# Dealing a second MLP's hidden units unevenly: ten full blocks of w2 and three more on 32 partitions

## The chip, the cores and the metric

The kernel runs on one core of a Trainium2 chip. The metric is the time of one execution on the device in microseconds, the median over runs. Before the change it was 671.67 us, from three runs between 671.4 and 671.77.

## The reference

One token passes through two identical pairs of layers, attention over a cache and then an MLP, all in float32. Both pairs use the same weights and the same cache.

```
D, F = 512, 1376;  H, S, Dh = 32, 4096, 128
attention(x): q = (x @ wq) as 32 heads of 128
              p = softmax(q . k_cache / sqrt(128)), over 4096 keys
              return (p . v_cache, heads joined) @ wo
mlp(x):       h = gelu(x @ w1 + b1)      # 512 -> 1376
              return h @ w2 + b2         # 1376 -> 512
x = x + attention(layernorm(x));  x = x + mlp(layernorm(x))     # twice
```

Each cache is 32 x 4096 x 128 floats, 67 MB. They are read for each layer, save for what stays on the chip between the two layers, so 285 MB cross from HBM in one execution.

## The kernel before

The 32 heads are eight groups of four. For a group the kernel loads a block of K (128 partitions x 16384 floats), one of V of the same size and a pair of weight tiles. They go to one large tile `arena`, in which three homes of 32 blocks of U = 512 columns (`A_AT`, `C_AT`, `B_AT`) are used in turn. All loads are issued on SP's queue by `load` (L108), in program order. The first layer takes the groups upwards, the second downwards.

Each transfer from SP signals its landing on one of eight semaphores, taken in turn (`DMAHW0` to `DMAHW7` in the orders below), so a transfer also waits until the one eight places before it has landed. TensorE's matmuls are held in program order by `matmul` (L113), and nearly all of them have this line in the profile.

A vector for TensorE stands as a column on the partitions. The 1376 hidden units of the MLP are four bands of `FJ` = 344, and band j is made on partitions 32j of a PSUM tile: in `mlp` (L334), for each of the four row blocks c of w1 and each band j, one matmul of 344 columns (L340). Its two output rows are the products with x and the sums of w1's columns, from which the layer norm is made good afterwards. A transpose in blocks of 32 (L353) turns each band so that its units stand on 32 partitions, 11 columns of them: unit 32c + r of band j is on partition 32j + r, column c. A band of 344 fills ten columns and 24 units of the eleventh, so 8 of 352 places are padding with zeros in w2 and b1. Two vector instructions and a gelu on ScalarE (L358 to L362) give `g`, 128 x 11, and then 11 blocks of w2 follow, each 128 partitions x 512 columns: block c is multiplied by column c of g in four matmuls of 128 columns, one for each quarter of the outputs (L365 to L368), accumulated in PSUM.

Padding in w2 is loaded with it: 128 rows of 11 x 2 KB, 2816 KB.

`idle` (L199) issues a matmul by zeros, with no use for its result; a 512-column one stands behind the gelu's inputs and one behind the fourth block of w2 (L374).

At the program's end, after the last group's V, SP issues wo, w1 in three transfers (`W1_AT_END`) and w2 in four (`W2_AT_END`: blocks 0 to 3, 4 to 7, 8 and 9, 10), L583 to L587. The destination is home A, w2 from its block 11 on. TensorE then makes the attention's output, w1's products as they land, and w2's products as they land; a last transpose (L184), an addition (L593) and a store of 2 KB (L594) end the program. The first MLP, in the middle of the program, runs through the same function with its own transfers and with fillers of its own.

Of the kernel before, what the change touches and what calls it, by code (L numbers as in the profile page):

```python
# [14 lines left out]
ALU = mybir.AluOpType  # L15
AX = mybir.AxisListType

P = 128
D = 512
H, S, DH = 32, 4096, 128  # L20
F = 1376
G = 8
J = 4
C = 8
FJ = F // J
FB = 11
W1C = FJ * J
EPS = 1e-5
U = 512
NC = 4 * U  # L30
# [7 lines left out]
A_AT, B_AT, C_AT = RING  # L38
# [4 lines left out]
SCRATCH = SHARED + 10 * U  # L43
# [11 lines left out]
W1_AT_END = ((0, 2), (2, 3), (3, 4))  # L55
LAST = ((0, 4), (4, 6), (6, 7), (7, 8))
W2_AT_CHANGE = (0, W1C, 2 * W1C, 3 * W1C, 10 * U, 11 * U)
W2_AT_END = (0, 4 * U, 8 * U, 10 * U, 11 * U)


@with_exitstack
def decode_layers(ctx: ExitStack, tc: tile.TileContext, vectors, k, v, w, w1, w2, out):
    nc = tc.nc
# [3 lines left out]
    def ctile(name, *shape):  # L67
        return const.tile([P, *shape], F32, name=name)
# [6 lines left out]
    cells = ctile("cells", CELLS)  # L75
# [3 lines left out]
    gelu = WIDE + 33  # L79
# [5 lines left out]
    def small(name, n=1):  # L85
        nonlocal first_front, rest
        if name.startswith("gelu_"):
            i = "hug".index(name[-1])
            return cells[:, gelu + FB * i : gelu + FB * (i + 1)]
        if name not in places:  # L90
            fit = [j for j in range(J) if gaps[j] + n <= ends[j]]
            if name in ("by_dma", "ready", "m"):
                places[name] = front, first_front, n
                first_front += n
            elif fit:
                places[name] = cells, gaps[fit[0]], n
                gaps[fit[0]] += n
            else:
                places[name] = cells, rest, n
                rest += n  # L100
        t, a, m = places[name]
        assert m == n and first_front <= FRONT and rest <= CELLS
        return t[:, a : a + n]

    def at(first, n):
        return arena[:, first : first + n]

    def load(first, src):  # L108
        t = at(first, src.shape[-1])
        tc.keep_in_program_order(nc.sync.dma_start(t, src))  # L110
        return t

    def matmul(*a, **kw):  # L113
        tc.keep_in_program_order(nc.tensor.matmul(*a, **kw))  # L114

    def activation(*a, **kw):
        tc.keep_in_program_order(nc.scalar.activation(*a, **kw))  # L117
# [14 lines left out]
    wq_t = by_four(load(SHARED, of_w(1, 0, 1)))  # L132
    nc.vector.memset(wide, 1.0)
    nc.vector.memset(cells[:, WIDE:], 0.0)
    by_dma = small("by_dma", FB + 8)
    b1c, b2c, xcol = by_dma[:, :FB], by_dma[:, FB : FB + 4], by_dma[:, FB + 4 :]
    nc.scalar.dma_start(by_dma, vectors)

    make_identity(nc, ident)
# [9 lines left out]
    pS, pO = (psum.tile([P, 512], F32, name=n) for n in ("pS", "pO"))  # L149
# [10 lines left out]
    zero = zq[:, :4]  # L160
# [4 lines left out]
    def of_32(t, n, i=0):  # L165
        return t[:, : 32 * n].rearrange("p (c q) -> p c q", q=32)[:, :, i]
# [4 lines left out]
    def pairs(t):  # L171
        return t[:, :8].rearrange("p (c i) -> p c i", i=2)
# [23 lines left out]
                nc.gpsimd.tensor_copy(pairs(t[:, 32 * j :])[:, :, 0], x)  # L196
        return t, s

    def idle(to, n=U, of=C_AT, amid=False):  # L199
        matmul(to[:, :n], zero[:, 0:1].to_broadcast([P, P]), at(of, n), start=not amid, stop=not amid)  # L200

    def idle_aside(n):
        for _ in range(n):
            idle(pM[:, ASIDE:], U - ASIDE)
# [6 lines left out]
    def mean_of(xs, s):  # L211
        nm = minus_mean(s, 0)
        xc, sq, ss, negm = small("xc", 4), small("sq", 4), small("ss"), small("negm")
        nc.vector.tensor_scalar(xc, pairs(xs)[:, :, 0], nm, None, op0=ALU.add)
        nc.vector.scalar_tensor_tensor(sq, xc, 1.0, xc, op0=ALU.mult, op1=ALU.mult, accum_out=ss)
        nc.vector.tensor_copy(negm, nm)
        return negm, ss

    def rstd_of(ss):
        nv = minus_mean(ss, 1)  # L220
        ve, r = small("ve"), small("rstd")
        nc.vector.tensor_scalar(ve, nv, -1.0, EPS, op0=ALU.mult, op1=ALU.add)
        if pM is pS:
            nc.vector.memset(pS[:, U - 2 :], 0.0)
        nc.gpsimd.tensor_tensor(r, ve, power, op=ALU.pow)
        return r
# [104 lines left out]
    def get_ready_for(function):  # L331
        activation(small("ready"), one, function)

    def mlp(xs, s, w1_t, w2_t, load_w2=None, behind_w2=None):  # L334
        get_ready_for(AF.Gelu_apprx_tanh)
        xb = small("xb", 4)
        nc.gpsimd.tensor_tensor(xb, pairs(xs)[:, :, 0], b2c, op=ALU.add)
        for c in range(4):
            for j in range(J):
                matmul(pO[32 * j : 32 * j + 2, :FJ], pairs(xs)[:, c, :], w1_t[c][:, FJ * j : FJ * (j + 1)],  # L340
                       start=(c == 0), stop=(c == 3))
            if c == 0:
                nm, ss = mean_of(xs, s)
            if c == 1:
                r = rstd_of(ss)
            if load_w2:
                load_w2(c)
                for _ in range(min(c + 1, 2) if c < 3 else 0):
                    idle(pO[:, 3 * P :], P, amid=True)
        if pS is not pO:  # L350
            idle(pS)
        ht = at(SCRATCH, 32 * FB)
        nc.vector.transpose(ht, pO[:, : 32 * FB])  # L353
        if pS is pO:
            idle_aside(2)
            idle(pO, U // 2)
        h, u, g = (small(f"gelu_{i}", FB) for i in "hug")
        nc.vector.scalar_tensor_tensor(h, of_32(ht, FB, 1), nm, of_32(ht, FB), op0=ALU.mult, op1=ALU.add)  # L358
        if load_w2:
            load_w2(4)  # L360
        nc.vector.scalar_tensor_tensor(u, h, r, b1c, op0=ALU.mult, op1=ALU.add)
        activation(g, u, AF.Gelu_apprx_tanh)  # L362
        if load_w2:
            get_ready_for(AF.Exp)
        for c in range(FB):  # L365
            for j in range(J):
                matmul(pS[32 * j : 32 * j + 1, :P], g[:, c : c + 1], w2_t[c][:, P * j : P * (j + 1)],
                       start=(c == 0), stop=(c == FB - 1))  # L368
            if load_w2:
                behind_w2(c)  # L370
                if c in (4, 7):
                    idle(pO[:, P:], U // 2, amid=True)
            elif c == 3:
                idle(pO)  # L374
        return of_32(turned(pS), 4), xb

    def load_w1(first, a, b):
        load(first + W1C * a, w1[:, W1C * a : W1C * b])

    def load_w2(first, a, b):  # L380
        load(first + a, w2[:, a:b])

    def in_rows(first, n, rows):
        return [at(first + n * i, n) for i in range(rows)]
# [7 lines left out]
    xs, s = set_x(zero, 1.0, xcol)  # L392
# [62 lines left out]
    for g in range(G):  # L455
# [4 lines left out]
        if g == G - 2:  # L460
            nc.scalar.copy(at(KEPT_K, KEPT * U), at(k_home + NC * C - KEPT * U, KEPT * U))
            pK.append(pS)
            pS = pO
# [6 lines left out]
        for c, t in blocks(v, g, v_home, LAST if final else ((0, C),)):  # L470
# [5 lines left out]
            if g == G - 2:  # L476
                for j in range(J):
                    i = 4 * c + j - KEPT_V // U
# [6 lines left out]
        if final:  # L485
# [3 lines left out]
            own = head_out(rl, wo_t, last=True, home=ident, clear=U // 2)  # L489
# [6 lines left out]
    x1, s1 = set_x(own, 1.0, acc, queries=False)  # L496
# [9 lines left out]
    def behind_w2(c):  # L506
# [7 lines left out]
        if c == 9:  # L514
            begin_k(SHARED + 2 * NC, 2)

    own, xb = mlp(x1, s1, in_rows(SHARED, W1C, 4), in_rows(SHARED, U, FB),
                  lambda i: load_w2(SHARED, *W2_AT_CHANGE[i : i + 2]), behind_w2)
    xs, s = set_x(own, 1.0, xb)
    g = G - 2  # L520
# [5 lines left out]
    for c in range(C):  # L526
        scores(z, c, quarters(C_AT + NC * c))
        if c == 0:
            nc.scalar.copy(at(C_AT, U), pM)
            nc.scalar.copy(at(C_AT + ASIDE, U - ASIDE), tail)  # L530
            pM, pO = pS, pK.pop()
# [19 lines left out]
    for i, first in enumerate([SHARED, SHARED + U] + [PAIR + U * j for j in range(4)]):  # L551
        t = at(first, U)
# [14 lines left out]
    for n in range(2, G):  # L567
        g, final = G - 1 - n, n == G - 1
        k_home, v_home = homes[(2 * n - 1) % 3], homes[2 * n % 3]
        acc, pt, rl = group(z, acc, ahead, blocks(k, g, k_home, HALVES if final else ((0, C),)),  # L570
                            C - 1 if final else C - 2, change_banks=final)
        if not final:
            by_pe = BY_PE_AT_BEGIN if n == 2 else BY_PE
            partly(pt, blocks(v, g, v_home, ((0, 6), (6, 8)) if n == 2 else ((0, C),)), v_home, by_pe)
            pair = load(PAIR, of_w(g % 2, g - 1, 2))
            z = next_queries(xs, negm, by_four(pair[:, :NC]), to=pS)
            ahead = added(v_home, by_pe), rl, by_four(pair[:, NC:])
            continue
        for c, t in blocks(v, g, v_home, LAST):
            values(c, pt, t, c)  # L580
            if c in (5, 7):
                idle(pS)
        wo_t = by_four(load(PAIR, of_w(g % 2, g, 1)))  # L583
        for a, b in W1_AT_END:
            load_w1(A_AT, a, b)
        for a, b in zip(W2_AT_END, W2_AT_END[1:]):
            load_w2(A_AT + 11 * U, a, b)  # L587
        own = head_out(rl, wo_t, last=True)
        idle(pO)
    x1, s1 = set_x(own, 1.0, acc, queries=False)  # L590
    own, xb = mlp(x1, s1, in_rows(A_AT, W1C, 4), in_rows(A_AT + 11 * U, U, FB))
    y = small("y", 4)
    nc.vector.scalar_tensor_tensor(y, own, 1.0, xb, op0=ALU.mult, op1=ALU.add)  # L593
    nc.sync.dma_start(out, y)  # L594
# [2 lines left out]
def columns(a):  # L597

    return np.ascontiguousarray(a.reshape(J, 4, 32, -1).transpose(0, 2, 1, 3).reshape(P, 4, -1))
# [36 lines left out]
```

## Time and profile before

| | |
|---|---|
| median of runs | 671.67 us |
| profiled execution | 671.53 us |
| its span, first to last instruction | 669.8 us |
| mean granted TensorE clock | 0.804 |
| read from HBM | 285.35 MB, 426 GB/s over the span |
| busy: TensorE matmul, VectorE, ScalarE, GpSimd | 57%, 56%, 4%, 1% |

A profile page gives the busy time of each engine, the span in 40 equal slices with one digit for the share of each (9 is 90% or more), the DMA queues, the chain of waits followed back from the end, and groups of instructions with the idle time before them. PE is TensorE's matmul and PEld its loading of weights; a matmul of float32 stands as two records of each. Of the DMA queues, q1 is that of SP's transfers, and q8 and q14 bring instructions. A view by stretches gives busy time per engine in chosen stretches, the granted clock, the mean busy share of the 16 DMA engines and GB/s. Times on the timeline are from the span's start; a name in brackets behind an instruction tells what ended the idle time before it.

### The profile page before, as it was taken

The numbers are of one execution on the slowest core, as the hardware profiler recorded it, in microseconds if no ns is written. First come the engines' busy times: TensorE is split into PE (matmuls) and PEld (weight loads), VectorE is DVE, ScalarE is ACT, GpSimd is POOL, SyncE is SP. The second block draws the span as 40 slices with busy tenths as digits, with TensorE's granted clock in tenths as the row PEclk, the third lists the DMA queues.
The fourth block names the chain that finished last, engine by engine and source line by source line (L and its number), as shares of the span: only waits on it lengthen the run. The fifth ranks groups of instructions, "written<-read, shape, count | busy, mean of one in ns | idle before, by whom it ended". The sixth has DMA issues, their size and how long they took to land.

```text
span 669.8 us, 5573 instructions
## 1 busy us (share of the span) xinstructions
PE 382.2 (57%) x2356; PEld 109.6 (16%) x2356; DVE 372.5 (56%) x474; ACT 29.7 (4%) x59; POOL 4.9 (1%) x23
## 2 busy tenths in 40 slices
PE   3441742636618446276778978627516456186686
PEld 1010110101101101011214222102101111021122
DVE  2049478395693965942212221492893966938831
ACT  0010000000000000002011120000000000000010
POOL 1000000000000000000000000000000000000000
PEclk9567875876778858787979999977859767786699
DMA  9999999999999999999999999999999999999996
GB/s 384 431 438 439 435 438 438 403 467 432 438 431 410 436 434 440 438 431 416 433 418 408 432 448 424 442 435 435 434 438 401 457 439 438 427 432 411 434 420 275
DMA packets 11544, 285.70 MB, mean 427 GB/s; under 512 B 1536, under 2 KB 1536, under 8 KB 3968
## 3 DMA queue, kind: packets, MB, share of 16 engines
q1 hardware_dynamic: 11376, 285.35, 99.0%
q8 instruction: 18, 0.29, 0.2%
q14 instruction: 6, 0.05, 0.0%
q10 hardware_dynamic: 144, 0.01, 0.0%
HBM read 285.35 MB, written 0.00 MB: 426 GB/s over the span
## 4 chain that ended last, share of the span: by engine, by line
DMA 62%; PE 28%; DVE 5%; another core or an unknown queue 2%; issue 1%; SPq 1%; ACT 0%; POOL 0%; DVEq 0%; ACTq 0%
DMA arena<-in_k 32%; DMA arena<-in_v 20%; PE pO L114 14%; PE pS L114 13%; DMA arena<-in_w 9%; DVE arena L280 3%; SPq L110 1%; DMA front<-in_vectors 1%; DVE arena L180 0%; ACT arena L117 0%; DVE arena L302 0%; PE pS L260 0%; DVE arena L184 0%; DVE cells L246 0%
## 5 line engine op out<-in xcount | busy, mean ns | idle before, releaser
L280 DVE TENSOR_TENSOR arena<-arena 128x2048 f32<-128x2048 f32 (+4 forms) x44 | 260.7, 5924 | 18.1 <-DMA arena<-in_v 17.3
L114 PE MATMUL pS<-arena,front 128*8 128x512 f32 (+2 forms) x466 | 72.6, 728 | 103.9 <-DMA arena<-in_k 103.9
L114 PE MATMUL pO<-arena,front 128*8 128x512 f32 (+3 forms) x602 | 86.1, 672 | 74.3 <-DMA arena<-in_k 49.0
L114 PE MATMUL pO<-arena,cells 128*128 128x512 f32 (+4 forms) x384 | 79.5, 462 | 21.6 <-DMA arena<-in_w 8.0
L114 PE MATMUL pS<-arena,cells 128*1 128x128 f32 (+3 forms) x320 | 58.4, 429 | 12.7 <-DMA arena<-in_w 9.7
L114 PE MATMUL pO<-arena 128*4 128x512 f32 x288 | 48.5, 806 | 19.9 <-DMA arena<-in_v 18.2
L302 DVE STREAM_TRANSPOSE arena<-pO 128x512 f32<-128x512 f32 x9 | 6.5, 717 | 63.6 <-PE pO L114 63.6
L114 PEld LDWEIGHTS pO<-arena,front 128*8 128x8 f32 (+1 forms) x602 | 19.3, 101 | 134.8 <-DVE arena L280 64.3
L114 PEld LDWEIGHTS pS<-arena,front 128*8 128x8 f32 (+1 forms) x466 | 15.0, 106 | 159.2 <-DVE arena L280 96.9
L180 DVE STREAM_TRANSPOSE arena<-pO 32x128 f32<-32x128 f32 x60 | 18.7, 312 | 39.3 <-PE pO L114 38.1
L114 PEld LDWEIGHTS pO<-arena,cells 128*128 128x128 f32 (+3 forms) x384 | 28.9, 122 | 69.9 <-issue 47.2
L114 PE MATMUL pS<-arena 128*4 128x512 f32 x216 | 32.2, 747 | 8.6 <-DMA arena<-in_v 7.4
L114 PEld LDWEIGHTS pS<-arena,cells 128*1 128x1 f32 (+3 forms) x320 | 23.1, 118 | 55.6 <-issue 42.9
L302 DVE STREAM_TRANSPOSE arena<-pS 128x512 f32<-128x512 f32 x7 | 5.0, 717 | 42.2 <-PE pS L114 42.2
L180 DVE STREAM_TRANSPOSE arena<-pS 32x128 f32<-32x128 f32 x48 | 15.0, 312 | 22.1 <-PE pS L114 21.0
L246 DVE TENSOR_REDUCE cells<-pO 128x1 f32<-128x512 f32 x9 | 6.2, 692 | 29.3 <-PE pO L114 29.2
L260 PE MATMUL pO<-front,arena 128*128 128x128 f32 x36 | 6.6, 313 | 25.1 <-ACT arena L117 25.1
L117 ACT ACTIVATE arena<-pO,cells 128x512 f32<-128x512 f32 x9 | 7.0, 779 | 268.8 <-DVE cells L251 268.8
L246 DVE TENSOR_REDUCE cells<-pS 128x1 f32<-128x512 f32 x7 | 4.8, 692 | 19.7 <-PE pS L114 19.5
L114 PEld LDWEIGHTS pO<-arena 128*4 128x4 f32 x288 | 7.8, 99 | 48.4 <-issue 40.4
L117 ACT ACTIVATE arena<-pS,cells 128x512 f32<-128x512 f32 x7 | 5.4, 778 | 231.8 <-DVE cells L251 231.8
L260 PE MATMUL pS<-front,arena 128*128 128x128 f32 x28 | 4.9, 304 | 18.6 <-ACT arena L117 18.6
(75 smaller groups left out, 105.0 us busy)
## 6 DMA issues: line engine op xcount, KB each, us to landing
arena<-in_w SPq DMA_DIRECT2D x13, 2048.0 KB, 11.7
arena<-in_k SPq DMA_DIRECT2D x4, 4096.0 KB, 25.2
arena<-in_v SPq DMA_DIRECT2D x2, 4096.0 KB, 39.7
arena<-in_w SPq DMA_DIRECT2D x9, 688.0 KB, 23.7
arena<-in_v SPq DMA_DIRECT2D x3, 2048.0 KB, 43.9
arena<-in_v SPq DMA_DIRECT2D x1, 6144.0 KB, 29.5
arena<-in_w SPq DMA_DIRECT2D x5, 1024.0 KB, 21.4
arena<-in_v SPq DMA_DIRECT2D x4, 1024.0 KB, 47.0
```

The source lines that it names most:

```text
L110: tc.keep_in_program_order(nc.sync.dma_start(t, src))
L114: tc.keep_in_program_order(nc.tensor.matmul(*a, **kw))
L117: tc.keep_in_program_order(nc.scalar.activation(*a, **kw))
L180: turn = nc.vector.transpose(t[q], src[q, P * j : P * (j + 1)])
L246: nc.vector.tensor_reduce(ml[:, 0:1], pS, axis=AX.X, op=ALU.max)
L260: tc.keep_in_program_order(nc.tensor.transpose(pT[:, b].rearrange("p j r -> p (j r)"), p[:, P * b : P * (b + 1)], ident))
L280: tc.keep_in_program_order(nc.vector.tensor_tensor(*a, **kw))
L302: nc.vector.transpose(ot, pO)
```

## The change

The units are dealt to the bands differently: bands 0, 1 and 2 have 352 units each, which is 11 full columns of 32, and band 3 the remaining 320, ten columns. No place in the first ten columns is padding. What stands in the eleventh column are 96 units on the first three bands.

In the first MLP this is all: the w1 products are 352, 352, 352 and 320 columns wide, and the eleventh block of w2 is multiplied on 96 partitions instead of 128.

In the second MLP the three eleventh columns are put side by side on partitions 0 to 31, as columns 10, 11 and 12. So w1 has six products for each row block: 352 columns for band 0, 320 for each of the others, and twice 32 columns that write the eleventh columns of bands 1 and 2 behind band 0's. The transpose is 416 columns wide, and g has 13 columns. The products with w2 begin with the three blocks on 32 partitions and go on with the ten on 128. In HBM, w2 has rows of 13 x 512 floats. Its last three blocks are loaded on 32 partitions alone, with four transfers of eight rows of 6 KB: partitions 0, 4, ... 28, then 1, 5, ... 29, and so on. They are issued behind w1 and ahead of the other blocks, which come in four transfers as before, now blocks 0 to 3, 4 to 7, 8, and 9.

The zeroing of PSUM behind w1 is done in the second MLP by the filler matmul ahead of it, which now opens the accumulation (`stop=False`), and w1's products all add to it.

```diff
-FJ = F // J
 FB = 11
-W1C = FJ * J
+FQ = 32 * FB
+FULL = 10
+MORE = 3
+W1C = F
@@
-W2_AT_END = (0, 4 * U, 8 * U, 10 * U, 11 * U)
+W2_AT_END = (0, 4 * U, 8 * U, 9 * U, 10 * U)
@@ in mlp
+        n = FB if load_w2 else FULL + MORE
+        if load_w2:
+            columns = [(j, 0, FQ * j, min(FQ, F - FQ * j)) for j in range(J)]
+            products = [(c, P) for c in range(FULL)] + [(FULL, 32 * MORE)]
+        else:
+            columns = [(0, 0, 0, FQ)] + [(j, 0, FQ * j, 32 * FULL) for j in range(1, J)]
+            columns += [(0, 32 * (FULL + j), FQ * j + 32 * FULL, 32) for j in range(1, MORE)]
+            products = [(FULL + j, 32) for j in range(MORE)] + [(c, P) for c in range(FULL)]
         for c in range(4):
-            for j in range(J):
-                matmul(pO[32 * j : 32 * j + 2, :FJ], pairs(xs)[:, c, :], w1_t[c][:, FJ * j : FJ * (j + 1)],
-                       start=(c == 0), stop=(c == 3))
+            for j, to, first, m in columns:
+                matmul(pO[32 * j : 32 * j + 2, to : to + m], pairs(xs)[:, c, :], w1_t[c][:, first : first + m],
+                       start=(c == 0 and n == FB), stop=(c == 3 and (j > 0 or n == FB or first == columns[-1][2])))
...
-        for c in range(FB):
+        for i, (c, k) in enumerate(products):
             for j in range(J):
-                matmul(pS[32 * j : 32 * j + 1, :P], g[:, c : c + 1], w2_t[c][:, P * j : P * (j + 1)],
-                       start=(c == 0), stop=(c == FB - 1))
+                matmul(pS[32 * j : 32 * j + 1, :P], g[:k, c : c + 1], w2_t[c][:k, P * j : P * (j + 1)],
+                       start=(i == 0), stop=(i == n - 1))
@@ at the end
         for a, b in W1_AT_END:
             load_w1(A_AT, a, b)
+        more = at(A_AT + 11 * U + FULL * U, MORE * U)
+        for i in range(4):
+            tc.keep_in_program_order(nc.sync.dma_start(more[i:32:4], w2[i:32:4, FULL * U :]))
         for a, b in zip(W2_AT_END, W2_AT_END[1:]):
             load_w2(A_AT + 11 * U, a, b)
         own = head_out(rl, wo_t, last=True)
-        idle(pO)
+        idle(pO, stop=False)
```

SP's queue at the end of the program, before. The rows of in_w are wo (2048 columns), w1 (2752 and twice 1376) and w2; in brackets the semaphores that a transfer waits for.

```order
L110 DMA arena<-in_v 128x2048 [waits PE_49]
L110 DMA arena<-in_w 128x2048 [waits DMAHW7_49,DMAHW0_49,PE_49]
L110 DMA arena<-in_w 128x2752
L110 DMA arena<-in_w 128x1376 [waits DMAHW1_49,PE_49]
L110 DMA arena<-in_w 128x1376 [waits DMAHW2_49,PE_49]
L110 DMA arena<-in_w 128x2048 [waits DMAHW3_49,PE_49]
L110 DMA arena<-in_w 128x2048 [waits DMAHW4_49]
L110 DMA arena<-in_w 128x1024 [waits DMAHW5_49]
L110 DMA arena<-in_w 128x512 [waits DMAHW6_49]
L594 DMA out<-cells 128x4 [waits DMAHW7_49,DVE_49]
```

The same place after the change.

```order
L112 DMA arena<-in_v 128x2048 [waits PE_49]
L112 DMA arena<-in_w 128x2048 [waits DMAHW7_49,DMAHW0_49,PE_49]
L112 DMA arena<-in_w 128x2752
L112 DMA arena<-in_w 128x1376 [waits DMAHW1_49,PE_49]
L112 DMA arena<-in_w 128x1376 [waits DMAHW2_49,PE_49]
L598 DMA arena<-in_w 8x1536 [waits DMAHW3_49,DVE_49]
L598 DMA arena<-in_w 8x1536 [waits DMAHW4_49]
L598 DMA arena<-in_w 8x1536 [waits DMAHW5_49]
L598 DMA arena<-in_w 8x1536 [waits DMAHW6_49]
L112 DMA arena<-in_w 128x2048 [waits DMAHW7_49,PE_49]
L112 DMA arena<-in_w 128x2048 [waits DMAHW0_49]
L112 DMA arena<-in_w 128x512 [waits DMAHW1_49]
```

The four small transfers have taken the semaphores 3 to 6, which w2's pieces had; those now wait for semaphores 7 and 0 to 2, which are those of wo and w1.

TensorE from w1's last two row blocks to the end of the program, before (pO holds w1's products, pS the others).

```order
L114 MATMUL pO<-arena,cells 2x344 x8
L114 MATMUL pS<-arena,front 128x512
L114 MATMUL pS<-arena,cells 1x128 x16
L114 MATMUL pO<-arena,front 128x512
L114 MATMUL pS<-arena,cells 1x128 x28
```

The same place after the change.

```order
L116 MATMUL pO<-arena,cells 2x352
L116 MATMUL pO<-arena,cells 2x320 x3
L116 MATMUL pO<-arena,cells 2x32 x2
L116 MATMUL pS<-arena,front 128x512
L116 MATMUL pS<-arena,cells 1x128 x28
L116 MATMUL pO<-arena,front 128x512
L116 MATMUL pS<-arena,cells 1x128 x24
```

Each row block of w1 has six products instead of four (the rows show the last one), 12 products of w2 have come ahead of the first 16, and of those behind the second filler 24 are left of 28.

More of the change, by code (lines that the diff above doesn't have):

```diff
@@ L88, in small @@
             i = "hug".index(name[-1])
-            return cells[:, gelu + FB * i : gelu + FB * (i + 1)]
+            return cells[:, gelu + (FULL + MORE) * i :][:, :n]
         if name not in places:
@@ L134, in decode_layers @@
     nc.vector.memset(cells[:, WIDE:], 0.0)
-    by_dma = small("by_dma", FB + 8)
-    b1c, b2c, xcol = by_dma[:, :FB], by_dma[:, FB : FB + 4], by_dma[:, FB + 4 :]
+    by_dma = small("by_dma", FULL + MORE + 8)
+    xcol, b2c, b1c = by_dma[:, :4], by_dma[:, 4:8], by_dma[:, 8:]
     nc.scalar.dma_start(by_dma, vectors)
@@ L197, in set_x, with idle @@
         return t, s
-    def idle(to, n=U, of=C_AT, amid=False):
-        matmul(to[:, :n], zero[:, 0:1].to_broadcast([P, P]), at(of, n), start=not amid, stop=not amid)
+    def idle(to, n=U, of=C_AT, amid=False, stop=True):
+        matmul(to[:, :n], zero[:, 0:1].to_broadcast([P, P]), at(of, n), start=not amid, stop=stop and not amid)
     def idle_aside(n):
@@ L351, in mlp @@
             idle(pS)
-        ht = at(SCRATCH, 32 * FB)
-        nc.vector.transpose(ht, pO[:, : 32 * FB])
+        ht = at(SCRATCH, 32 * n)
+        nc.vector.transpose(ht, pO[:, : 32 * n])
         if pS is pO:
@@ L356, in mlp @@
             idle(pO, U // 2)
-        h, u, g = (small(f"gelu_{i}", FB) for i in "hug")
-        nc.vector.scalar_tensor_tensor(h, of_32(ht, FB, 1), nm, of_32(ht, FB), op0=ALU.mult, op1=ALU.add)
+        h, u, g = (small(f"gelu_{i}", n) for i in "hug")
+        nc.vector.scalar_tensor_tensor(h, of_32(ht, n, 1), nm, of_32(ht, n), op0=ALU.mult, op1=ALU.add)
         if load_w2:
             load_w2(4)
-        nc.vector.scalar_tensor_tensor(u, h, r, b1c, op0=ALU.mult, op1=ALU.add)
+        nc.vector.scalar_tensor_tensor(u, h, r, b1c[:, :n], op0=ALU.mult, op1=ALU.add)
         activation(g, u, AF.Gelu_apprx_tanh)
@@ L588, in decode_layers @@
         own = head_out(rl, wo_t, last=True)
-        idle(pO)
+        idle(pO, stop=False)
     x1, s1 = set_x(own, 1.0, acc, queries=False)
-    own, xb = mlp(x1, s1, in_rows(A_AT, W1C, 4), in_rows(A_AT + 11 * U, U, FB))
+    own, xb = mlp(x1, s1, in_rows(A_AT, W1C, 4), in_rows(A_AT + 11 * U, U, FULL + MORE))
     y = small("y", 4)
@@ L604 @@
         x=A_x, k=A_k_cache, v=A_v_cache, wq=A_wq, wo=A_wo, w1=B_w1, b1=B_b1, w2=B_w2, b2=B_b2).items()}
-    pad = 32 * FB - FJ
-    w2 = np.pad(a["w2"].reshape(J, FJ, D), ((0, 0), (0, pad), (0, 0)))
-    b1 = np.pad(a["b1"].reshape(J, FJ), ((0, 0), (0, pad)))
+    b1, w2 = (np.pad(t, ((0, J * FQ - F), (0, 0))).reshape(J, FB, 32, -1).transpose(0, 2, 1, 3)
+              for t in (a["b1"][:, None], a["w2"]))
+    b1, w2 = (np.concatenate((t.reshape(P, FB, -1),) + tuple(
+        np.pad(t[j, :, FULL:], ((0, P - 32), (0, 0), (0, 0))) for j in range(1, MORE)), axis=1).reshape(P, -1)
+        for t in (b1, w2))
     wq = columns(a["wq"]).reshape(P, 4, G, J, J, 32)
@@ L616 @@
     arrays = dict(
-        vectors=np.concatenate((b1.reshape(J, FB, 32).transpose(0, 2, 1).reshape(P, FB),
-                                columns(a["b2"])[:, :, 0], columns(a["x"])[:, :, 0]), axis=1),
+        vectors=np.concatenate((columns(a["x"])[:, :, 0], columns(a["b2"])[:, :, 0], b1), axis=1),
         k=apart(a["k"].reshape(G, J, C, U, DH).transpose(0, 4, 2, 1, 3).reshape(G, P, BLOCK)),
@@ L621 @@
         w=apart(np.array(w).transpose(0, 2, 1, 3).reshape(2, P, G * NC)),
-        w1=columns(a["w1"]).reshape(P, 4 * J * FJ),
-        w2=w2.reshape(J, FB, 32, D).transpose(0, 2, 1, 3).reshape(P, FB * D),
+        w1=columns(a["w1"]).reshape(P, 4 * F),
+        w2=w2,
     )
```

## The prediction

> **What bounds the kernel now.** I read the page from the top, then the stretches at the end, then the last instructions in order of time.
>
> ```profile
> span 669.8 us, 5573 instructions
> DMA  9999999999999999999999999999999999999996
> DMA packets 11544, 285.70 MB, mean 427 GB/s; under 512 B 1536, under 2 KB 1536, under 8 KB 3968
> q1 hardware_dynamic: 11376, 285.35, 99.0%
> q8 instruction: 18, 0.29, 0.2%
> DMA 62%; PE 28%; DVE 5%; another core or an unknown queue 2%; issue 1%; SPq 1%; ACT 0%; POOL 0%; DVEq 0%; ACTq 0%
> ```
>
> The DMA engines are full in 39 of 40 slices: the loads set the pace, and only the last slice shows 6. The program has 79 transfers from SP, all of 128 rows, and 11376 is 79 x 144: each transfer is 128 packets, one for each row whatever its length, and 16 more, one for each engine. A row is never divided. I need the last slice in detail.
>
> ```profile
> core 0: us, PE busy (x) PEld busy (x) DVE busy (x) ACT busy (x) POOL busy (x), PEclk, DMA share, GB/s
> 654.00:658.00 4.00, 2.82 (x24) 0.84 (x20) 0.93 (x7) 0.00 (x0) 0.20 (x1) 1.00 1.01 422
> 662.00:663.00 1.00, 0.67 (x27) 0.67 (x30) 0.00 (x0) 0.00 (x0) 0.00 (x0) 1.00 0.88 363
> 663.00:664.00 1.00, 1.00 (x18) 0.39 (x6) 0.00 (x0) 0.00 (x0) 0.00 (x0) 1.00 0.67 270
> 664.00:665.00 1.00, 0.75 (x14) 0.30 (x16) 0.00 (x0) 0.00 (x0) 0.00 (x0) 1.00 0.38 148
> 665.00:666.00 1.00, 0.84 (x32) 0.53 (x26) 0.00 (x0) 0.00 (x0) 0.00 (x0) 1.00 0.12 47
> ```
>
> The last two columns are the mean busy share of the 16 engines and what they moved. The engines don't end together: from 662 to 666 the share falls from 0.88 to 0.12, and 0.12 of 16 is two engines, which alone work on through 665 to 666. They get no faster for being alone: 422 GB/s over 16 x 1.01 is 26.1 GB/s an engine, 47 over 16 x 0.12 is 24.5. So what counts is not the sum of bytes but the bytes of the two engines that end last. A transfer has landed when its slowest engine is done.
>
> ```profile
> 659.55 0.76 PE L114 MATMUL pO<-arena,cells 128*2 128x344 f32 x8 [0.44 <-DMA arena<-in_w]
> 660.24 1.12 PE L114 MATMUL pS<-arena,front 128*128 128x512 f32 x2
> 660.38 0.55 DVE L353 STREAM_TRANSPOSE arena<-pO 128x352 f32<-128x352 f32 x1 [1.63 <-PE pO L114]
> 661.64 0.21 ACT L117 ACTIVATE cells<-cells 128x11 f32<-128x11 f32 x1 [19.93 <-DVE cells L361]
> 662.33 1.05 PE L114 MATMUL pS<-arena,cells 128*1 128x128 f32 x32 [0.97 <-DMA arena<-in_w]
> 663.32 1.12 PE L114 MATMUL pO<-arena,front 128*128 128x512 f32 x2
> 664.69 1.05 PE L114 MATMUL pS<-arena,cells 128*1 128x128 f32 x32 [0.25 <-DMA arena<-in_w]
> 665.90 1.01 PE L114 MATMUL pS<-arena,cells 128*1 128x128 f32 x24 [0.16 <-DMA arena<-in_w]
> 666.51 0.10 PEld L114 LDWEIGHTS pS<-arena,cells 128*1 128x1 f32 x8 [0.29 <-DMA arena<-in_w]
> 666.98 0.32 DVE L184 STREAM_TRANSPOSE arena<-pS 128x128 f32<-128x128 f32 x1 [5.43 <-PE pS L114]
> 667.52 0.35 SPq L594 DMA_DIRECT2D out<-cells  x1
> ```
>
> Four times TensorE waits for a piece of w2: products start at 662.33 (16 matmuls, two records each), 664.69 (16), 665.90 (8) and 666.51 (4). From the last landing to the store is 1 us that the change leaves alone. Where there is data, 16 matmuls take 1.05 us, 0.066 each.
>
> **The change part by part.** *Bytes.* The eleventh block of w2, 128 rows of 2 KB, goes: 8 rows or 16,384 B an engine, 0.63 us at 26.1 GB/s. Four transfers of 8 rows of 6 KB come, ahead of the other blocks. No row above shows a transfer of fewer than 128 rows, so I bound how they spread. Above, a row is a packet and packets are whole, so eight rows can't occupy more than eight engines; a spread over all 16 (12 KB each, 0.16 us less on every engine) is excluded. The other end is one engine: 196,608 B, 7.5 us, less 0.63. I take eight engines with one row each, nearest to the rows of 128, where every engine has an equal share. If the same eight take all four, each has 24,576 B more, 0.94 us, and ends 0.31 later than now; the other eight end 0.63 earlier. The padding saved, 64 KB, is 0.15 us at 427 GB/s, but the split decides. The Trainium skill, "DMA: Bandwidth & Descriptors", "Why a DMA increments its semaphore by 16 and not by 1", says that a copy uses the largest number up to 16 that divides the outer sizes, on the lowest-numbered engines: eight here, the same eight four times. No run so far shows it.
>
> *Issue.* SP issues four more transfers, each about 0.33 us. Transfers take eight completion semaphores in turn, and one waits for the transfer eight before it. So the four small ones take over the waits for the pieces of v, and the four pieces of w2 now wait for wo and the three pieces of w1.
>
> ```profile
> L110 SPq DMA_DIRECT2D arena<-in_w x2: 327/380/433, 616.6 to 617.0; - x2
> DMA to landing us min/median/max: 36.3/37.7/39.2
> L110 SPq DMA_DIRECT2D arena<-in_w x2: 328/352/377, 634.2 to 634.6; - x2
> DMA to landing us min/median/max: 23.7/24.3/24.9
> L110 SPq DMA_DIRECT2D arena<-in_w x1: 328/328/328, 650.5 to 650.5; - x1
> DMA to landing us min/median/max: 16.0/16.0/16.0
> out<-cells SPq DMA_DIRECT2D x1, 2.0 KB, 1.4
> ```
>
> Wo and the first of w1 land near 652.9 and 656.2, the others near 657.9 and 659.5. The last piece of w2, now issued at 650.5 with 16.0 us to go, is issued near 659.6. A transfer with nothing ahead lands in 1.4 us (the store), so its rows are ready by 661.0. The first engines end near 662.5 (the share in 662 to 663 is still 0.88) with 0.63 us for the last block, so they reach it about 661.8: no gap, with 0.8 us to spare. Even a gap there falls on engines that have 3.5 us of slack. I take 0, with 1.4 us (all of that latency laid bare on the last engines) as the far end.
>
> *TensorE.* Each of the four row blocks of w1 has six products in place of four: two more, 32 columns wide, while the widest goes from 344 to 352. Nearest are the products at 0.066: 0.13 us behind the last piece of w1. The transpose is of 416 columns, 0.55 x 416/352 = 0.65, 0.10 more. So the gelu ends up to 0.23 later than 661.85, about 662.1. Then 12 products on the first 32 partitions (a quarter of the rows, the same 128 columns: 0.79 us) come ahead of the first piece. Eight more small matmuls than now stand between gelu and end.
>
> *First MLP and the rest.* Its four w1 products are 352, 352, 352 and 320 wide in place of 344, the last block has 96 rows, and nothing is issued differently: nearest, 0.76 us for four of 344, so 0.02 us for each block. I take 0; loads hide it, and bare it is 0.1.
>
> *The sum, if the two last engines are among the eight that are loaded.* Landings of the first two pieces of w2 come 0.94 later, the last one 0.31 later, near 666.8. TensorE has its 12 small products and the 16 of the first piece done (663.3 + 1.05), and the 512-column filler, by 665.4. The second piece lands near 665.6; from there 24 matmuls without a break, 1.57, end at 667.2, where now the last four end near 666.51 + 0.26 = 666.8. That is +0.31 by the loads and +0.4 by TensorE behind them. The profiled execution took 671.53 (span 669.8 and 1.7 around it), 0.14 under the median of the runs. 671.53 + 0.37 = 671.9.
>
> **The rivals.** *The last two are among the other eight.* Then the loads end 0.3 to 0.6 earlier. For: nothing in the profile names an engine. Against: drawn blind, both lie in one given half in 8 x 7 / (16 x 15) = 23% of draws. What it gives is taken by TensorE: 662.3, 12 products to 663.1, 16 to 664.15, the filler of 1.05 to 665.2, 16 to 666.25, eight to 666.8, the same end as now. 671.5. The wait for loads gives way to a queue of products. The same holds if the eight rows were to be spread evenly.
>
> The Trainium skill, same page, "Latency and other measured facts", says that engines 7 and 15 are usually slower. By that rule one of the two last is loaded, and the time is the forecast's; two late engines agree with it, while which they are no row shows.
>
> *Small transfers hold up their ring.* If each occupied an engine for its whole latency, 1.4 us as the store's, instead of its packets' time, four would add 5.6 to the loaded engines in place of 0.94: 671.5 + 5.6 - 0.63 = 676.5, slower. It decides as soon as a transfer costs over 0.6. Against it: shares of 1.01 while w1 and w2 follow each other in pieces of 256 to 1024 KB. For: none there is as small. The Trainium skill, same page, "Rules for kernel authors", says that under 64 KB a transfer is mostly overhead; these are 48 KB. No row shows whether that overhead is hidden behind a full ring.
>
> *The new places of the tensors or of the instruction blocks move the lag.* The 18 instruction packets of 16 KB each hold one engine for some 0.6 us (16,384 B at 26.1 GB/s), on whichever engine they fall. 64 more records on TensorE's queue may shift the last one to another engine: +0.6 or -0.6, 672.1 or 670.9.
>
> **How the numbers follow.** The forecast (two or one of the last engines loaded) 0.58; the other half, or an even spread, 0.30; small transfers that cost 0.05; shifted blocks 0.07. Likeliest: 671.9. The range takes in the first two with the runs' own spread (671.4 to 671.77) and half the shift: 671.0 to 672.5. A measurement of this kernel tells about 0.2%, 1.3 us, from no change. Both main cases lie within it, so within 0.2% is 0.92; slower by more, the small transfers and a laid-bare issue, 0.06; faster by more 0.02, for the change takes away at most 0.63 us from any engine.
>
> **What would show it.** Packets of q1: 79 x 144 + 4 x (8 + 8) = 11440 if eight engines share a small transfer, 11412 if one does. The shares at the end fall in a step of about eight engines, near 661.8 to 664, if the last engines are loaded; if not, all end nearer together. The wait before the last four products becomes short, that before the second piece longer. The 12 small products stand right behind the gelu. Wrong would be an end set by w1 or by gelu, q1 idle before 661, or a time beyond 672.5.

## The result, and the profile after

The changed kernel takes 679.18 us (median of 4 runs, 678.58 to 679.42) against 671.59 before: a ratio of 1.0112, 95% interval 1.0094 to 1.0129. It is 7.6 us slower, and outside the range of the prediction.

The time is not lost in the loads. This is the view by stretches of the kernel after, with the same columns as in the prediction (busy time of PE, PEld, DVE, ACT and POOL, then granted clock, DMA share, GB/s).

```profile
650.00:654.00 4.00, 2.10 (x10) 0.41 (x10) 0.72 (x1) 0.00 (x0) 0.00 (x0) 1.00 1.01 427
654.00:658.00 4.00, 0.00 (x0) 0.00 (x0) 0.00 (x0) 0.00 (x0) 0.00 (x0) 0.90 1.02 425
658.00:660.00 2.00, 0.00 (x0) 0.00 (x0) 0.33 (x2) 0.00 (x0) 0.00 (x0) 0.50 1.00 420
664.00:665.00 1.00, 1.00 (x15) 0.52 (x14) 0.00 (x0) 0.00 (x0) 0.00 (x0) 0.98 0.31 115
665.00:666.00 1.00, 1.00 (x15) 0.52 (x15) 0.44 (x4) 0.00 (x0) 0.00 (x0) 1.00 0.05 18
666.00:668.00 2.00, 2.00 (x27) 1.10 (x28) 0.40 (x3) 0.00 (x0) 0.55 (x1) 1.00 0.00 0
```

The DMA engines are as full as before, and in this execution they end earlier: the share in 665 to 666 is 0.05 where it was 0.12. But from 654 to 659.6 no compute engine does anything, and TensorE works on until 673.7, long after the last load. The timeline shows what it waited for (start, duration, engine, line; in brackets the idle time before and its end).

```profile
651.74 0.72 DVE L304 STREAM_TRANSPOSE arena<-pO 128x512 f32<-128x512 f32 x1 [9.29 <-PE pO L116]
659.64 0.18 DVE L308 TENSOR_REDUCE cells<-arena 128x4 f32<-128x16 f32 x1 [7.18 <-DMA arena<-in_w]
659.85 0.23 DVE L310 TENSOR_SCALAR cells<-cells 128x4 f32<-128x4 f32 x1
660.14 1.89 PE L116 MATMUL pS<-arena,cells 128*1 128x128 f32 x32 [7.41 <-DVE cells L310]
661.95 2.08 PE L116 MATMUL pO<-arena,front 128*128 128x512 f32 x2
669.41 1.82 PE L116 MATMUL pS<-arena,cells 32*1 32x128 f32 x56 [0.58 <-ACT cells L119]
672.22 1.49 PE L116 MATMUL pS<-arena,cells 128*1 128x128 f32 x48
674.32 0.35 SPq L607 DMA_DIRECT2D out<-cells  x1
```

L308 is the sum over the last head's values, in `head`. It stood at 652.39 before (there it is L306), right behind its transpose, and the products of wo and the filler followed:

```profile
652.39 0.18 DVE L306 TENSOR_REDUCE cells<-arena 128x4 f32<-128x16 f32 x1
653.05 1.05 PE L114 MATMUL pS<-arena,cells 128*1 128x128 f32 x32 [0.42 <-DMA arena<-in_w]
654.03 1.12 PE L114 MATMUL pO<-arena,front 128*128 128x512 f32 x2
```

Now it waits 7.18 us for a transfer of in_w. It needs nothing from w1 or w2. The order of the two programs, with what each instruction waits for, has the reason, on VectorE:

```
before:  L306 TENSOR_REDUCE cells<-arena 128x4 [waits DVE_49]
after:   L308 TENSOR_REDUCE cells<-arena 128x4 [waits DMAHW5_49,DMAHW4_49,DMAHW6_49,DMAHW3_49,DVE_49]
```

DMAHW3 to DMAHW6 are the four small transfers. They write columns 10752 to 12287 of `arena`; the reduction reads 16 values of each partition, every 32nd column in four groups that lie 129 apart, from the scratch place at column 50688. They have no byte in common. The layer that puts the waits into the program took the two accesses to overlap. The small transfers lie in the queue behind w1's last piece, so the wait runs until about 659.5, and everything from the attention's output to the store is behind it on VectorE and TensorE.

The sum over the two profiled executions, of 671.53 and 678.58 us: the reduction starts 7.25 us later (659.64 against 652.39), and the store 6.80 later (674.32 against 667.52). So what comes behind the reduction takes 14.68 where it took 15.13. It gains the waits for w1 and w2, which have landed by the time that TensorE comes to them. It loses by TensorE's granted clock, which falls to 0.50 in the idle time: 16 products of wo take 1.89 us instead of 1.05 and the filler behind them 2.08 instead of 1.12, 1.80 together. And the added products stand bare in it, since no wait for loads hides them.

### The profile page after: what moved, and what is told of

The parts are those of the page before. It is cut to its first block, busy times and chain, and to the rows that moved or that the text cites. A ratio compares the mean times of both kernels' runs of the same rounds, so it can differ in the third digit from the quotient of the medians.

```text
span 676.8 us, 5645 instructions
## 1 busy us (share of the span) xinstructions
PE 391.7 (58%) x2388; PEld 114.2 (17%) x2388; DVE 372.3 (55%) x474; ACT 29.6 (4%) x59; POOL 4.8 (1%) x23
## 3 DMA queue, kind: packets, MB, share of 16 engines
q1 hardware_dynamic: 11440, 285.29, 98.0%
## 4 chain that ended last, share of the span: by engine, by line
DMA 62%; PE 28%; DVE 5%; another core or an unknown queue 2%; issue 1%; SPq 1%; ACT 0%; POOL 0%; DVEq 0%; ACTq 0%
DMA arena<-in_k 28%; DMA arena<-in_v 22%; PE pO L116 15%; PE pS L116 13%; DMA arena<-in_w 12%; DVE arena L282 3%; SPq L112 1%; DMA front<-in_vectors 1%; DVE arena L182 0%; ACT arena L119 0%; DVE arena L186 0%; DVE arena L304 0%; DVE cells L248 0%; DVE arena L363 0%
## 5 line engine op out<-in xcount | busy, mean ns | idle before, releaser
L116 PE MATMUL pO<-arena,front 128*8 128x512 f32 (+3 forms) x602 | 89.3, 690 | 73.4 <-DMA arena<-in_k 47.9
L116 PE MATMUL pO<-arena,cells 128*128 128x512 f32 (+7 forms) x400 | 81.2, 454 | 19.0 <-POOL cells L198 6.5
L116 PE MATMUL pS<-arena,cells 128*1 128x128 f32 (+4 forms) x336 | 64.3, 447 | 18.7 <-DVE cells L310 8.7
L116 PE MATMUL pO<-arena 128*4 128x512 f32 x288 | 46.4, 782 | 21.7 <-DMA arena<-in_v 19.5
L116 PEld LDWEIGHTS pO<-arena,cells 128*128 128x128 f32 (+4 forms) x400 | 30.3, 122 | 68.9 <-issue 47.6
L116 PEld LDWEIGHTS pS<-arena,cells 128*1 128x1 f32 (+4 forms) x336 | 25.9, 126 | 64.9 <-issue 46.9
```

## The experiments

Three theories were tried. Theory W: the false wait of the reduction is the loss. Theory R: transfers of eight rows hold up the loads. Theory P: TensorE's added products are the loss. All ratios are to the kernel before in the same comparison (671.59 for the change, 671.45 to 671.50 for the others).

| run | us | ratio, 95% interval |
|---|---|---|
| the change | 679.18 | 1.0112 (1.0094 to 1.0129) |
| blocks8 | 673.19 | 1.0022 (1.0013 to 1.0032) |
| one32 | 672.85 | 1.0021 (1.0012 to 1.0030) |
| behind | 671.35 | 1.0000 (0.9991 to 1.0009) |
| own_tile | 671.58 | 1.0003 (0.9994 to 1.0012) |
| lone | 677.35 | 1.0083 (1.0069 to 1.0097) |
| lone_behind | 671.71 | 1.0003 (0.9994 to 1.0012) |
| warm | 677.32 | 1.0090 (1.0076 to 1.0104) |
| near_behind | 672.77 | 1.0020 (1.0011 to 1.0029) |
| finer | 672.39 | 1.0014 (1.0005 to 1.0024) |
| own_mid | 672.14 | 1.0008 (0.9999 to 1.0017) |

**behind: the same transfers, recorded behind the reduction.**

```diff
-        more = at(...); for i in range(4): dma(more[i:32:4], w2[i:32:4, FULL * U :])
-        for a, b in zip(W2_AT_END, W2_AT_END[1:]): load_w2(A_AT + 11 * U, a, b)
         own = head_out(rl, wo_t, last=True)
+        more = at(...); for i in range(4): dma(more[i:32:4], w2[i:32:4, FULL * U :])
+        for a, b in zip(W2_AT_END, W2_AT_END[1:]): load_w2(A_AT + 11 * U, a, b)
```

> The change with its strided transfers as they are, but recorded behind the last head's sum in the program, so that they wait for that reduction and not it for them. Theory W: L308 near 652.4 and 671.5 to 672.3; the first strided transfer is issued near 652.7 in place of 642, with some 7 us of loads still ahead of it in the queue, so nothing runs dry. Theory R and P: 679, the transfers and the matmuls are the same.

Measured 671.35, a little under what W gave.

```profile
652.44 0.18 DVE L308 TENSOR_REDUCE cells<-arena 128x4 f32<-128x16 f32 x1
```

All the added products and transfers are there, and the whole loss is gone. That decides for W against R and P.

**own_tile: the three small blocks in a tile of their own.** The same effect, without moving the transfers in the queue.

```diff
-ARENA = KEPT_K + KEPT * U
+ARENA = KEPT_K
+    kept = ctile("kept", KEPT * U)          # also where L471 and L548 keep three blocks of K
-        more = at(A_AT + 11 * U + FULL * U, MORE * U)
+        more = kept
```

> The change with the three small blocks in a tile of their own (the 1536 columns that hold three blocks of K between the layers) in place of the large tile. Partitions four apart, the same four transfers issued at the same time, the same matmuls; the program then has no wait of L308 for them. Theory W: L308 near 652.4, 671.0 to 671.8. Of the prediction's two cases: if the engines that end last are among the loaded eight, the last piece of w2 lands near 666.8 and the time is 671.7 or more; if they are among the others it lands near 665.8, TensorE's queue of 12 + 16 + filler + 24 products ends where it ended before, and the time is 671.2 to 671.6.

Measured 671.58, no different from before. The transfers step over partitions as in the change and are issued from 640.9 to 650.6 (642.2 to 650.6 in the change); the reduction has no wait for them and runs at 652.50. Its timeline:

```profile
662.15 0.83 PE L117 MATMUL pS<-kept,cells 32*1 32x128 f32 x24 [0.58 <-ACT cells L120]
662.92 1.05 PE L117 MATMUL pS<-arena,cells 128*1 128x128 f32 x32
663.90 1.12 PE L117 MATMUL pO<-arena,front 128*128 128x512 f32 x2
665.21 1.63 PE L117 MATMUL pS<-arena,cells 128*1 128x128 f32 x48 [0.18 <-DMA arena<-in_w]
666.44 0.10 PEld L117 LDWEIGHTS pS<-arena,cells 128*1 128x1 f32 x8 [0.26 <-DMA arena<-in_w]
667.45 0.35 SPq L608 DMA_DIRECT2D out<-cells  x1
```

This is what the change does without the false wait. The store is issued at 667.45, where it was 667.52. Four waits of TensorE's products for pieces of w2 have become one of 0.18 us, and behind it the last 24 products stand in one row, though the weights of the last four still wait 0.26 us for the last piece.

**lone and lone_behind: the wait alone.** The kernel before, with one transfer of eight rows that nobody reads.

```diff
+        more = at(A_AT + 11 * U + FB * U, 3 * U)
+        dma(more[0:32:4], w2[0:32:4, : 3 * U])   # lone: ahead of w2's loads;
         for a, b in zip(W2_AT_END, W2_AT_END[1:]):
             load_w2(A_AT + 11 * U, a, b)
-        own = head_out(rl, wo_t, last=True)      # lone_behind: this ahead of all of it
```

> The kernel before, with one added transfer of eight rows of 6 KB on partitions 0, 4, ... 28 between w1 and w2, into a place that nobody reads. No change to the MLPs. Theory W: the last head's reduction waits until that transfer has landed, near 659, so 677 to 679. Theory R: one quarter of the loss, 673.5. Theory P: no loss beyond the bytes, 671.6 to 672.0.

> The run lone, with its one transfer recorded behind the last head's sum. Theory W: the reduction is at 652.4 again and the time 671.4 to 672.1, some 0.2 us of bytes on eight engines over the kernel before. If a strided transfer costs something of its own, it stays above 673.

Measured 677.35 and 671.71. One transfer of 48 KB costs 5.9 us when the reduction is recorded behind it, and no measurable time when it is recorded ahead. In lone the wait is the same as in the change:

```profile
659.75 0.18 DVE L306 TENSOR_REDUCE cells<-arena 128x4 f32<-128x16 f32 x1 [7.16 <-DMA arena<-in_w]
673.11 0.35 SPq L596 DMA_DIRECT2D out<-cells  x1
```

From w1's first product to the store lone takes 9.30 us (663.81 to 673.11), the change 10.36 (663.96 to 674.32). So theory P has a part in the loss, but only behind the wait: 1.1 us for the added products and the wider transpose, which cost no measurable time in own_tile and in behind.

**warm: TensorE busy through the wait.** Eight 512-column fillers ahead of `head_out`.

```diff
+        for _ in range(8):
+            idle(pS)
         own = head_out(rl, wo_t, last=True)
```

> The change as it is, wait and all, with eight more 512-column filler matmuls ahead of the last head's sum, which TensorE makes while it waits. Theory W with the clock (TensorE's clock fell to 0.50 in the wait, and 16 products took 1.89 us in place of 1.05, a filler 2.08 in place of 1.12): granted clock 1.00 from 658 on and 677.2 to 678.2, 1 to 2 us less than the change. If the clock has no part in the loss: 679.2.

Measured 677.32 (676.71 to 679.12 over four runs), at the median 1.9 us less than the change, with the wait still there.

```profile
658.00:660.00 2.00, 2.00 (x6) 0.84 (x5) 0.41 (x2) 0.00 (x0) 0.00 (x0) 1.00 1.02 425
659.48 0.18 DVE L308 TENSOR_REDUCE cells<-arena 128x4 f32<-128x16 f32 x1 [5.99 <-DMA arena<-in_w]
660.56 1.05 PE L116 MATMUL pS<-arena,cells 128*1 128x128 f32 x32
661.54 1.12 PE L116 MATMUL pO<-arena,front 128*128 128x512 f32 x2
672.94 0.35 SPq L609 DMA_DIRECT2D out<-cells  x1
```

The granted clock stays at 1.00, and the products of wo are at 1.05 again. Of the 1.80 that the two rows lost, 0.42 goes to the fillers, which hold these products back from 660.14 to 660.56, and the store comes 1.38 earlier. So 1.4 to 1.9 of the 7.6 us are a clock that fell because TensorE had nothing to do.

**blocks8 and one32: neighbouring partitions.**

```diff
-            dma(more[i:32:4], w2[i:32:4, FULL * U :])                       # four times
+            dma(more[8 * i : 8 * i + 8], w2[8 * i : 8 * i + 8, FULL * U :])  # blocks8
+        dma(more[:32], w2[:32, FULL * U :])                                 # one32, once
```

> The change, with each small transfer on eight neighbouring partitions (0 to 7, 8 to 15, ...) in place of eight partitions four apart. Sizes, places in the queue and matmuls are the same; in the program the last head's reduction (L308) then waits for no transfer. Theory W (the time was lost in that reduction's wait for the four small transfers, 7.2 us): 671.5 to 672.1, with L308 near 652.4 again and the loads, not TensorE, ahead of each product. Theory R (eight-row transfers hold up the loads): stays at 679. Theory P (more matmuls behind w1 and the gelu): stays at 677 to 679, since they are all still there.

> The change, with one transfer of 32 neighbouring rows for the three blocks. Theory W: no wait at L308, 671.3 to 671.9. If rows go to engines evenly (two each on 16), each engine has 4 KB less than before the change, and the DMA share at the end falls as it did before; against the run with eight neighbouring rows the last landing should be up to 0.5 us earlier if the last engines are among the eight loaded there, later if they are not. Theory R: between, about 674, as one small transfer in place of four. Theory P: 677 to 679.

Measured 673.19 and 672.85. The wait is gone in both, as W has it, but they are 1.8 and 1.5 us slower than behind, which W had not allowed for. The stretch in which the small transfers move shows why; one row of the view from each, blocks8, then one32, then own_tile with partitions four apart:

```profile
658.00:660.00 2.00, 1.56 (x26) 0.77 (x17) 0.34 (x4) 0.00 (x0) 0.55 (x1) 1.00 1.02 293
```

```profile
658.00:660.00 2.00, 1.53 (x23) 0.77 (x17) 0.31 (x4) 0.00 (x0) 0.55 (x1) 1.00 1.03 286
```

```profile
658.00:660.00 2.00, 1.88 (x31) 0.94 (x26) 0.32 (x4) 0.00 (x0) 0.55 (x1) 1.00 1.03 434
```

All engines are busy, but with neighbouring rows they move a third less. Packet by packet, each of the 32 rows of 6 KB took 0.234 us in own_tile and 0.234 to 0.441 in blocks8, and the rows of w2 that start between 655.5 and 661 took 0.411 at the median, in own_tile 0.309. w1's last piece, on which the row blocks of the second MLP wait, comes late with them: in blocks8 its products start at 660.85, in the kernel before at 659.55.

```profile
660.85 0.87 PE L116 MATMUL pO<-arena,cells 128*2 128x352 f32 x12 [1.29 <-DMA arena<-in_w]
```

**near_behind: partitions or the time of issue?** behind, with blocks8's partitions.

```diff
-            dma(more[i:32:4], w2[i:32:4, FULL * U :])
+            dma(more[8 * i : 8 * i + 8], w2[8 * i : 8 * i + 8, FULL * U :])
```

> The run behind, with neighbouring partitions in place of partitions four apart. Neither has the wait; they differ in the partitions alone, and are issued at the same time. Theory N (eight engines that write to neighbouring partitions get in each other's way, as the stretch of 293 GB/s at a full DMA share in blocks8 suggests): 672.6 to 673.4, the same dip between 658 and 660, w1's last piece over 1 us late. Theory T (blocks8 and one32 lost 1.5 us against behind because of when their transfers were issued): 671.4, no dip.

Measured 672.77, with 273 GB/s at a share of 1.03 in that stretch, and the same late w1. The expectation had them issued at the same times as in behind, and that was wrong: without the step they don't wait for VectorE either, and they went out at 640.8 to 650.5, as in blocks8 and own_tile. That makes own_tile its better partner: the same times of issue, partitions four apart, no dip, 671.58. And behind, with the later issue and partitions four apart, has no dip either (433 GB/s). So it is the partitions.

**finer and own_mid: is there a version that gains?** behind with w2 in pieces of 4, 3, 2 and 1 blocks and half the filler; own_tile with the 12 small products behind the fourth block in place of the filler.

```diff
-W2_AT_END = (0, 4 * U, 8 * U, 9 * U, 10 * U)
+W2_AT_END = (0, 4 * U, 7 * U, 9 * U, 10 * U)                              # finer
-                idle(pO)
+                idle(pO, U // 2)                                          # finer; own_mid drops it
+            products = [(c, P) for c in range(FULL)]                      # own_mid
+            products[4:4] = [(FULL + j, 32) for j in range(MORE)]
```

> The run behind, with w2's blocks in pieces of 4, 3, 2 and 1 in place of 4, 4, 1 and 1, and the filler after the fourth block half as long. In behind the last 24 products stood in one run behind the second piece's landing (665.66 to 667.30). If TensorE's queue is what sets the end there: products start some 0.6 us earlier and the time is 670.7 to 671.1. If the landing of the last piece sets it: 671.3, as behind.

> The run own_tile, with the 12 small products behind the fourth block, in the place of the 512-column filler there, which goes. If TensorE's queue is what holds back the earlier loads in own_tile: its last products start right at the last landing, near 665.8, and the time is 0.4 to 0.8 us less than own_tile's, 670.6 to 671.1. If the last landing sets the end in own_tile too: the same time.

Measured 672.39 and 672.14. Neither gains: finer missed both of its expected times and is a little slower than the kernel before, and own_mid doesn't show the 0.4 to 0.8 us. Their runs spread more (671.19 to 674.46, and 671.09 to 673.12) than those of the kernel before, as do own_tile's (671.14 to 673.35) and behind's (671.10 to 673.19), and in their profiled executions the last loads ended later than in own_tile's. Why they spread wasn't settled. In own_mid's profiled execution the engine that ended last, at 667.1, was one of the eight with the small rows; one execution doesn't tell whether that is the reason. No version tried is faster than the kernel before.

## Why the prediction was wrong, point by point

**The step that failed is the one on issue.** It asked what the four small transfers wait for, and what the transfers behind them wait for, and took 0 with 1.4 us as the far end. It didn't ask who waits for the four transfers, other than their own products. The orders shown ahead of the prediction are SP's and TensorE's; VectorE's is not among them, and its instructions don't move. Its waits do: the reduction has four more semaphores. A sign of it stood in SP's order, where the first small transfer waits for DVE_49, which no load of w1 or w2 did before. The price was in rows at hand: the transfers lie behind w1's last piece, whose landing was worked out as 659.5, against a reduction at 652.4. No rival had a wait on VectorE.

**The end of the loads: left open.** The forecast had the two last engines among the eight that are loaded, and the last piece landing 0.3 later than before, at 666.8; the rival had it 0.3 to 0.6 earlier. Before, it was issued at 650.5 and took 16.0, so it landed at 666.5. After:

```profile
L112 SPq DMA_DIRECT2D arena<-in_w x1: 327/327/327, 659.6 to 659.6; - x1
DMA to landing us min/median/max: 6.1/6.1/6.1
```

That is 665.7. But the change is no fair partner here, since its program is late: between 656 and 663 an instruction packet (q8) moves among the last loads in the kernel before, and none in the change. In own_tile and behind, which have no wait, such a packet is there again, and the last piece lands at 659.6 + 6.8 = 666.4 in own_tile and at 666.9 in behind:

```profile
L112 SPq DMA_DIRECT2D arena<-in_w x1: 328/328/328, 659.6 to 659.6; - x1
DMA to landing us min/median/max: 7.3/7.3/7.3
```

An engine's packets follow each other without a gap in the trace, so some can be followed to the end. In the change the last engine has none of the small rows and ends at 665.47, with a loaded one close ahead of it at 665.39. In lone_behind the last engine is a loaded one: its row of 6 KB at 659.13 is followed by 32 rows of w2 up to 666.16. So neither case held in all executions. The times lean to the rival's 671.5 (own_tile 671.58, behind 671.35), but both intervals take in the forecast's 671.9 too. The rival's reason, that TensorE's queue takes what the loads give, fits own_tile's timeline: the filler was to be over near 665.2 (663.90 + 1.12 = 665.02), the last products done near 666.8 (665.21 + 1.63).

**Shifted instruction blocks: not decided.** The rival took 0.6 us for an instruction packet; in the kernel before they took 0.88 to 0.97, and the change has 19 of them in place of 18. The last landings lie between 665.7 in the change and 667.4 in own_mid. How much of that is theirs wasn't followed.

**Eight engines, a row each: right.** q1 has 11440 packets, the number given for it, and one32, with 32 rows, 11424, which is 79 x 144 + 32 + 16, all 16 engines.

```profile
q1 hardware_dynamic: 11440, 285.29, 98.0%
```

```profile
q1 hardware_dynamic: 11424, 285.29, 99.1%
```

So the rule quoted from the Trainium skill, "DMA: Bandwidth & Descriptors", "Why a DMA increments its semaphore by 16 and not by 1", that eight rows go to eight engines, agrees with the trace. That the same eight are used each time shows in the packets of the change: the 32 rows of 6 KB form eight runs of four, each row starting within 4 ns of the end of the one before. Which of the 16 engines these are no run shows.

**The issue times: right for w2.** The last piece of w2 was issued at 659.6, as given, and the DMA share stayed at 1.00 to 1.05 until 662. A small transfer took SP 0.62 to 0.78 us to issue, not 0.33.

**First MLP: right.** Without the wait the reduction stands at 652.44 in behind and 652.50 in own_tile, against 652.39 before, so what lies ahead of it costs 0.1 us at most.

**Small transfers hold up their ring: wrong.** 676.5 lies nearest to the result by number, and that is chance: own_tile has the same four transfers and loses nothing.

**TensorE: right in size.** In own_tile the small products start at 662.15, right behind the gelu, as the working had it (662.1 and 662.3), and the 12 take 0.83 (0.79 given).

**Not in the list at all:** the step of four partitions is itself what keeps the small transfers cheap. The prediction never priced the partitions.

## What to carry to other kernels

When a transfer is added, list everything that waits for its landing, on all engines, from the program's own waits, before pricing it; an engine whose instructions don't move may have new semaphores. An access that steps over partitions can be taken for a conflict with another stepped access in the same tile though they share no byte: a tile of its own, or a recording order in which the other access comes first, takes the wait away. And where engines' idle time is put into a chain, add what the clock loses, here 1.4 to 1.9 us, and the products that the loads no longer hide, here 1.1.

## What the runs showed of the hardware that was not expected

Transfers to neighbouring partitions run at a lower rate with all engines busy: 273 to 293 GB/s in the stretch where eight or 32 neighbouring rows of 6 KB move, against 434 with rows four partitions apart, and 1.2 to 1.6 us of the kernel's time against own_tile. The Trainium skill, "SBUF — State Buffer", section "Door 1: The DMA port swizzle", says that four neighbouring partitions share a port on the DMA side, so that eight neighbours reach two ports and eight rows four apart reach eight. The trace agrees with that in direction, and for one32 too, where all 16 engines write 32 neighbours, which reach eight ports by that section; no run shows the ports themselves.

The step costs SP's queue instead. The first row is the four small transfers of the change, the second those of blocks8:

```profile
L598 SPq DMA_DIRECT2D arena<-in_w x4: 623/632/777, 642.2 to 650.6; - x4
```

```profile
L598 SPq DMA_DIRECT2D arena<-in_w x4: 272/274/345, 640.9 to 650.6; - x4
```

A stepped transfer of eight rows takes 0.63 us to issue, one of eight neighbours 0.27. The rows of the change move only from 655.5 on, behind the other loads, so it costs nothing here.
